# Linear attention beside a gated feed-forward: query features scaled to one normaliser before they are turned, and all sixteen numerators moved among the gate/up chunks

## The chip, the cores and the metric

The kernel runs on one core of one Trainium2 chip. The metric is the device time of one execution in microseconds (us); the median of several runs is what counts. A core has five engines that each work through their own instructions in order and wait for one another by semaphores: TensorE (PE in the profile; its weight loads are PEld), VectorE (DVE), ScalarE (ACT), GpSimd (POOL) and SyncE (SP, which here only issues DMAs). TensorE writes to PSUM, eight banks of 512 f32 columns on 128 rows; all else lives in SBUF, 128 rows as well.

## The reference

Input x is 2048 tokens by 640, bf16. Two branches are computed from it and mixed by a gate per token:

```
g = sigmoid((x * gate_w).sum(-1))
out = g * A(x) + (1 - g) * B(x)

A: q, k, v = x @ wqkv                         32 heads of 20
   pq = q @ w_phi[h],  pk = k @ w_phi[h]      20 x 20 per head
   phi(p) = [softmax(p), softmax(-p)]         40 features
   kv = sum over tokens of phi(pk)^T v        z = sum over tokens of phi(pk)
   o  = (phi(pq) @ kv) / (phi(pq) . z + 1e-6)
   A  = o @ wo                                640 x 640
B: (gelu(x @ w_gate) * (x @ w_up)) @ w_down   640 -> 1728 -> 640
```

The attention is linear: all keys go into one state of 40 x 20 per head, and each query then needs one product with this state (the numerator) and one with z (the normaliser).

## The kernel before, in words

Tokens are handled in 16 tiles of 128 and, for the feed-forward, in 4 blocks of 512. A small recorder (`_Sched.op`, `_Sched.dma`) issues every instruction in program order to its engine, and adds the semaphore waits that the named buffers need. So the order of work on each engine is the order in which the Python code calls the methods. All DMAs of weights and all transposing DMAs are issued by SP, in program order, on one queue.

**Loads and constants** (`loads`). x, the weights of v, and parts of the up weights are issued first. GpSimd fills masks and the constant columns: for each slot of the key features `Ek` (L294, L295) and of the query features `Eqt` (L297, L298) it writes ones at the last of each head's 20 columns and in the padding. The last feature's exponent is subtracted from the others beforehand, so it is always exp(0) = 1 and is never computed.

**Attention state** (`attention_state`). TensorE projects v, then folds `w_phi` into the k weights and the q weights (`fold`). The folded weights are evacuated from PSUM in slices by VectorE; slice 3 of the k weights and of the q weights goes over ScalarE to a staging buffer and from there by one GpSimd subtraction (`fold_stage`, L451) into place. After that come k projections (`k_tile`), k and q together (`kq_tile`), their exponentials on ScalarE (`exps`, L549), the norm of the key features on VectorE (`k_norm`: a reduction L628, a reciprocal L636, a product L637) and the sum over tokens on TensorE (`gram`, L646, eleven groups of three heads). The features lie in eleven groups of 128 columns; each group holds 64 columns of exp(p) and 64 of exp(-p), for three heads of 20 and 4 columns of padding. A tile's query features are written to `Eqt`, and a transposing DMA on SP's queue (L595) turns them at once into `Eq`, so that features lie on the rows. In between, SP issues the gate and up weights piece by piece, then the down weights and `wo`.

**Gate and up** (`ffn`, `gateup`). For each block of 512 tokens there are 14 chunks of hidden columns: ten matmuls of 512 columns (gate, then up), a gelu on ScalarE (L809) and a multiply on VectorE (L813). The narrow chunk 13 has gate and up in five matmuls. For the first block the up half of five chunks (2 to 6) has been computed ahead in the attention stage, so those chunks have only five matmuls. The last grams, the state (`kv_state`) and the gates of all tokens (`gates`) lie among the first four chunks. Two PSUM bank pairs, (0, 1) and (6, 7), take turns. In the last block, six chunks run in this form, in banks 2 to 5, and eight as half-row matmuls (`gateup_halves`, L832: 64 rows of the array for gate and 64 for up side by side, then swapped), with numerators 0, 1 and 2 between them.

**Numerators** (`num`). The state matrix `KV` has, for each group of three heads, 66 columns: 20 of kv, one of z and one of ones for each head. The two softmaxes are not yet normalised when the matmuls run, so the 64 rows of exp(p) and the 64 rows of exp(-p) go to two separate outputs: 22 half-row matmuls per tile (`num_mms`, L875). VectorE then has twelve steps per tile (`num_steps`): the ones columns give the two softmax sums; from these come the ratio, the normaliser, its reciprocal, the gate (L893 to L900), two products of 640 columns (L904) and their sum (L906). A transposing DMA (L909) turns the result into `goT`, eight slots.

**Down** (`down_pair`). For two tiles at a time TensorE multiplies hidden rows with `w_down` and the turned attention rows with `wo` (L935, half-row matmuls in pairs), and ScalarE scales the result by the gate (L948) ahead of the store. Numerators 3 to 15 lie between these matmuls, 13 in all.

## Time and profile before

| what | value |
|---|---|
| median of three runs | 282.25 us (281.9 to 282.58) |
| profiled execution, own time | 281.68 us |
| its span | 280.4 us, 7063 instructions |
| granted TensorE clock | 1.00 in every stretch |
| TensorE busy | 276.6 us (99%) |
| VectorE busy | 177.3 us (63%); 19.6 of 20 us from 40 to 80 us |
| ScalarE busy | 106.4 us (38%) |
| GpSimd busy | 14.4 us (5%), 69 instructions |
| attention stage, gate/up stage, down stage | up to 80, 80 to 193, 193 to 278.5 us |

The page has busy times per engine, the span in 40 slices, the DMA queues, the chain of work that ended last, and the costliest groups of instructions. A group's row reads: line, engine, operation, output <- inputs, shape, count | total busy us, mean ns of one | idle time of the engine before them and what ended it. A row of the chain in order of time reads: start, duration, engine, buffer and line, count. A row of the timeline reads: start, duration, engine, line, operation, and in brackets the idle time before it and its releaser. In the table of DMA issues the last number is the median time from issue to landing. Ends of matmuls are modelled, and the spans of GpSimd instructions are rough.

### The profile page before, as it was taken

What the parts mean: (1) busy time and instruction counts of PE and PEld (TensorE: products, weight loads), DVE (VectorE), ACT (ScalarE), POOL (GpSimd) and SP (SyncE); (2) the same over time, 40 slices, a digit from 0 to 9 for tenths busy, and PEclk for the clock granted to TensorE, in tenths of its full rate; (3) what the DMA queues carried; (4) which work ended last, traced back from release to release, by engine and by line L of the source; (5) the groups of instructions that cost most, each with busy time, mean ns of one, the idle gap of its engine ahead of it and who ended that gap; (6) DMA issues with size and microseconds to landing.
All of it is one profiled execution on the core that took longest, in us unless ns stands there. A gap on an engine that the chain in (4) does not pass through costs nothing.

```text
span 280.4 us, 7063 instructions
## 1 busy us (share of the span) xinstructions
PE 276.6 (99%) x2994; PEld 168.1 (60%) x3006; DVE 177.3 (63%) x342; ACT 106.4 (38%) x205; POOL 14.4 (5%) x69
## 2 busy tenths in 40 slices
PE   8999999999999999999999999999999999999997
PEld 4576766666765444444444444445777777777785
DVE  2666999999998524233242234878884883883801
ACT  3347877878783423222323223122112112112021
POOL 7411001101000000000000000000000000000000
DMA  7999069887899910000000000101133142232221
GB/s 217 224 220 189 6 136 165 171 163 146 162 191 273 347 41 0 2 0 0 1 2 0 0 0 2 23 2 26 26 50 108 35 76 56 62 59 66 71 75 47
DMA packets 59994, 24.11 MB, mean 86 GB/s; under 512 B 50874, under 2 KB 59450, under 8 KB 59962
## 3 DMA queue, kind: packets, MB, share of 16 engines
q1 hardware_dynamic: 59296, 23.63, 37.7%
q8 instruction: 23, 0.38, 0.6%
q10 hardware_dynamic: 666, 0.03, 0.2%
q14 instruction: 9, 0.07, 0.1%
HBM read 9.04 MB, written 2.62 MB: 42 GB/s over the span
## 4 chain that ended last, share of the span: by engine, by line
PE 97%; DMA 1%; issue 0%; SPq 0%; ACT 0%
PE ps L466 52%; PE ps L935 29%; PE ps L832 6%; PE ps L610 4%; PE ps L480 2%; PE ps L875 2%; PE ps L646 2%; DMA xtok<-in_A_x_dram 1%; PE ps L406 1%; PE ps L342 0%; SPq L230 0%; ACT outsb L948 0%; PE ps L371 0%
## 5 line engine op out<-in xcount | busy, mean ns | idle before, releaser
L809 ACT ACTIVATE gl<-ps 128x512 bf16<-128x512 f32 x52 | 31.1, 597 | 71.2 <-PE ps L466 56.3
L466 PE MATMUL ps<-xT,wu_sb 128*128 128x512 bf16 x214 | 52.9, 379 | 0.3
L466 PE MATMUL ps<-xT,wg_sb 128*128 128x512 bf16 x214 | 52.7, 379 | 0.3
L466 PE MATMUL ps<-w,xT 128*128 128x368 bf16 (+6 forms) x340 | 51.6, 303 | 0.0
L813 DVE TENSOR_TENSOR hT<-ps,gl 128x512 bf16<-128x512 f32 x34 | 23.4, 691 | 44.5 <-PE ps L466 44.5
L935 PE MATMUL ps<-wd_sb,hT 64*128 64x320 bf16 x648 | 48.2, 296 | 0.0
L948 ACT ACTIVATE outsb<-ps,Gm 128x320 bf16<-128x320 f32 (+2 forms) x31 | 14.6, 516 | 70.3 <-PE ps L935 70.3
L466 PEld LDWEIGHTS ps<-w,xT 128*128 128x128 bf16 x340 | 32.1, 98 | 14.6
L935 PEld LDWEIGHTS ps<-wd_sb,hT 64*128 64x128 bf16 x648 | 30.9, 94 | 11.8
L466 PEld LDWEIGHTS ps<-xT,wu_sb 128*128 128x128 bf16 x220 | 21.5, 98 | 25.6
L466 PEld LDWEIGHTS ps<-xT,wg_sb 128*128 128x128 bf16 x220 | 21.2, 98 | 25.2 <-issue 0.2
L935 PE MATMUL ps<-wo_sb,goT 64*128 64x320 bf16 (+2 forms) x340 | 26.5, 288 | 0.0
L628 DVE TENSOR_REDUCE Dk<-Ek 128x66 f32<-128x1320 bf16 x16 | 24.3, 1520 | 2.3 <-ACT gcol L539 2.3
L637 DVE TENSOR_TENSOR Ek<-Ek,Dk 128x1320 bf16<-128x1320 bf16 x16 | 24.5, 1533 | 0.5
L904 DVE TENSOR_TENSOR O<-ps,RH 128x640 bf16<-128x640 f32 x32 | 24.8, 815 | 0.0
L549 ACT ACTIVATE Ek<-ps 128x627 bf16<-128x627 f32 x32 | 20.5, 693 | 6.0 <-PE ps L610 4.5
L549 ACT ACTIVATE Eqt<-ps 128x627 bf16<-128x627 f32 x32 | 20.6, 704 | 2.4 <-PE ps L466 2.4
L935 PEld LDWEIGHTS ps<-wo_sb,goT 64*128 64x128 bf16 x340 | 15.8, 94 | 5.5
L832 PE MATMUL ps<-xT,wg_sb 64*128 64x512 bf16 x80 | 17.6, 376 | 0.0
L832 PE MATMUL ps<-xT,wu_sb 64*128 64x512 bf16 x80 | 17.6, 376 | 0.0
L935 PE MATMUL ps<-wd_sb,xT 64*128 64x320 bf16 (+2 forms) x270 | 16.0, 269 | 0.0
L893 DVE RECIPROCAL RH<-ps 128x32 f32<-128x32 f32 x16 | 5.7, 356 | 13.4 <-PE ps L875 13.4
(97 smaller groups left out, 222.3 us busy)
## 6 DMA issues: line engine op xcount, KB each, us to landing
out_dram<-outsb SPq DMA_DIRECT2D x7, 320.0 KB, 2.9
wd_sb<-in_B_w_down_dram SPq DMA_DIRECT2D x1, 2080.0 KB, 12.2
wg_sb<-in_B_w_gate_dram SPq DMA_DIRECT2D x5, 224.0 KB, 3.1
wg_sb<-in_B_w_gate_dram SPq DMA_DIRECT2D x5, 192.0 KB, 3.0
wu_sb<-in_B_w_up_dram SPq DMA_DIRECT2D x5, 192.0 KB, 3.9
wo_sb<-in_A_wo_dram SPq DMA_DIRECT2D x1, 800.0 KB, 10.2
xtok<-in_A_x_dram SPq DMA_DIRECT2D x2, 320.0 KB, 3.2
w<-in_A_wqkv_dram SPq DMA_DIRECT2D x4, 160.0 KB, 3.6
```

Source lines behind the costliest of these rows:

```text
L466: self.sc.op("pe", lambda e: e.matmul(self.ps[:, bank * 512 + c0:bank * 512 + c0 + n], lhs, rhs, start=first, stop=fin), reads=reads, writ ...
L549: self.sc.op("act", lambda e: e.activation(dst, src, AF.Exp, scale=scale), reads=[("ps", b), ("ps", b + 1)], writes=[(name, sl, s)])
L610: self.sc.op("pe", lambda e: e.matmul(out, self.xT[:, kt, t * P:(t + 1) * P], self.w3[:, kt, c:c + 2 * n].rearrange("p (r w) -> p r w", w= ...
L628: self.sc.op("dve", lambda e: e.tensor_reduce(self.Dk[:, se, 0, :].rearrange("p (u h) -> p u h", h=self.HG), self.k_view(se), AX.X, ALU.ad ...
L637: sc.op("dve", lambda e: e.tensor_tensor(v, v, R.rearrange("p (u h) -> p u h", h=self.HG).unsqueeze(3).to_broadcast([P, 2 * self.G, self.H ...
L809: self.sc.op("act", lambda e: e.activation(self.gl[:, slot, :], self.bank(bank), AF.Gelu_apprx_tanh), reads=[("ps", bank)], writes=[("gl", ...
L813: self.sc.op("dve", lambda e: e.tensor_tensor(self.hT(b, c), up, self.gl[:, slot, :], ALU.mult), reads=[upk, ("gl", slot)], writes=[("hT", ...
L832: sc.op("pe", lambda e: e.matmul(self.bank(bk), w[a:a + 64, kt, c * P:(c + 1) * P], self.xT[a:a + 64, kt, b * self.BT:(b + 1) * self.BT], ...
L893: dve(lambda e: e.reciprocal(R(0), Dn[1]), rb, [key(0)], guard=old)
L904: dve(lambda e, o=o, f=f, s=s: e.tensor_tensor(o, V[s][:, :, 0:DH], f, ALU.mult), rb[2 * s:2 * s + 2] + [key(6 + s)], [("O", s, sl)], guar ...
L935: sc.op("pe", lambda e: e.matmul(self.bank(bk, w), lhs, rhs, start=opens and x == 0, stop=end and not opens, skip_group_check=True), reads ...
L948: sc.op("act", lambda e: e.activation(dst, self.bank(bk, w), AF.Copy, scale=g), reads=rd, writes=wr)
```

## The change

The query features are no longer turned as they come, unnormalised. They stay in token rows, in a buffer `Eq` with a slot for each of the 16 tiles, and are scaled first: VectorE sums the two sets of 20 exponentials of each head (`q_sums`, two reductions of 660 elements), forms the ratio of the two sums (`q_ratio`: a reciprocal and a product of 33 columns), and GpSimd multiplies the exp(-p) half by this ratio (`q_scale`, 660 elements). Both halves then share one normaliser, and a group's 128 rows can go through one matmul. Then the transposing DMA turns the tile (`q_turn`): tile 0 into a buffer of its own (`Eq0`), tile t into the slot of tile t-1, which has been turned by then.

A numerator has eleven matmuls of 128 rows and 63 columns (the ones columns are gone from `KV`), in PSUM banks 2 and 3, and three VectorE steps: the normaliser, its reciprocal, and one product of 640 columns with gate and reciprocal, from which `goT` is turned. `goT` has twelve slots; the last four tiles use freed slots of `Eq`.

All 16 tiles are now handled inside the gate/up stage: counting chunks from 0 over all four blocks, sums, ratio and scale of tile t come behind chunk 3 + 3t, numerator t behind chunk 8 + 3t, and the turn of tile t+1 is issued just ahead of numerator t (that of tile 0 right behind its scale). From the seventh chunk on three bank pairs take turns. The half-row chunks and the numerators among the down matmuls are gone. GpSimd's constants for the queries become a fill of all 16 tiles of `Eq` with ones, 1408 columns each, in the order `QT` in which the tiles are projected, at the end of `loads`; the fills come ahead of both `fold_stage` instructions on its queue.

```diff
@@ class _Kernel
-    DB = DH + 2
+    DB = DH + 1
-    NEQ = 4
+    NSQ = 4
+    NGO = 12
+    QT = (0, 4, 1, 2, 3) + tuple(range(5, 16))
@@ alloc
-        self.Eq = T("Eq", [P, self.G, S], BF16)
+        self.Eq = T("Eq", [P, NT, self.G * P], BF16)
...
@@ loads
-        for s in range(self.NEQ):
-            pool(lambda e, s=s: e.memset(self.consts(self.Eqt, s, 0), 1.0), [("Eqtc", s)])
-            pool(lambda e, s=s: e.memset(self.consts(self.Eqt, s, 1), 1.0), [("Eqtp", s)])
+        for t in self.QT:
+            pool(lambda e, t=t: e.memset(self.Eq[:, t, :], 1.0), [("Er", t, 0), ("Er", t, 1)])
@@ q_rest
-        sl = self.nq % self.NEQ
-        self.nq += 1
-        self.exps(self.Eqt, sl, "Eqt", (b + 2) * 512 - (self.H * self.E - n))
-        self.sc.dma("sp", lambda e: e.dma_start_transpose(self.Eq[:, :, t * P:(t + 1) * P], self.Eqt[:, sl, :]),
-                    reads=[("Eqt", sl, 0), ("Eqt", sl, 1), ("Eqtc", sl), ("Eqtp", sl)], writes=[("Eq", t)])
+        self.exps(self.Eq, t, "Er", (b + 2) * 512 - (self.H * self.E - n))
+    def q_sums(self, t):
...
+        for s in (0, 1):
+            sc.op("dve", lambda e: e.tensor_reduce(
+                self.Dq[:, sl, s, :].rearrange("p (g h) -> p g h", h=HG), u[:, s], AX.X, ALU.add),
+                reads=[("Er", t, s)], writes=[("Dq", sl, s)], guard=old)
+    def q_ratio(self, t):
...
+        self.sc.op("dve", lambda e: e.reciprocal(b, b), writes=[("Dq", sl, 1)])
+        self.sc.op("dve", lambda e: e.tensor_tensor(b, a, b, ALU.mult), reads=[("Dq", sl, 0)], writes=[("Dq", sl, 1)])
+    def q_scale(self, t):
...
+        self.sc.op("pool", lambda e: e.tensor_tensor(
+            v, v, ratio.unsqueeze(3).to_broadcast([P, G, HG, self.DH]), ALU.mult),
+            reads=[("Dq", sl, 1)], writes=[("Er", t, 1)])
+    def turned(self, t):
+        return self.Eq[:, t - 1, :] if t else self.Eq0[:, :]
+    def q_turn(self, t):
+        self.sc.dma("sp", lambda e: e.dma_start_transpose(
+            self.turned(t).rearrange("p (g q) -> p g q", q=P), self.Eq[:, t, :]),
+            reads=[("Er", t, 0), ("Er", t, 1)], writes=[("Eq", t)],
+            guard=[("Er", t - 1, s) for s in (0, 1)] if t else ())
@@ kv_state
-        ones = KV[:, :, :, self.DH + 1]
-        sc.op("dve", lambda e: e.tensor_copy(ones, m.unsqueeze(1).to_broadcast([P, self.G, self.HG])),
-              reads=["hm"], writes=["KVd"])
-    def gateup_halves(self, b, cs, pairs, held):
...
@@ num
+        for g in range(self.G):
+            n, o = min(w, H * DB - w * g), base + w * g
+            sc.op("pe", lambda e: e.matmul(
+                self.ps[:, o:o + n], self.turned(t)[:, g * P:(g + 1) * P], self.KV[:, g, 0:n], start=True, stop=True),
+                reads=[("Eq", t)] + [(k, g0) for k in ("KV", "KVz") for g0 in (0, 8, 10)],
+                writes=[("ps", o // 512)], signal=g in (5, self.G - 1))
...
+        sc.op("dve", lambda e: e.scalar_tensor_tensor(
+            R(0), self.Dq[:, t % self.NSQ, 0, 0:H], 1e-6, V[:, :, DH], ALU.mult, ALU.add),
+              reads=rb + [("Dq", t % self.NSQ, 0)], writes=[key(0)], guard=old)
+        sc.op("dve", lambda e: e.reciprocal(R(1), R(0)), reads=[key(0)], writes=[key(1)], guard=old)
+        sc.op("dve", lambda e: e.scalar_tensor_tensor(
+            self.Og[:, sl, :].rearrange("p (h d) -> p h d", d=DH), V[:, :, 0:DH], self.Gr[:, t:t + 1],
+            R(1).unsqueeze(2).to_broadcast([P, H, DH]), ALU.mult, ALU.mult),
+            reads=rb + [key(1), "Gr"], writes=[("Og", sl)], guard=old)
...
@@ ffn
+        two, three = [(0, 1), (6, 7)], [(4, 5), (0, 1), (6, 7)]
         order = [0, 1, 13] + list(range(2, 13))
+        top, step = 8, 3
+        n = 0
+        for b in range(self.NB):
             for idx, c in enumerate(order):
+                self.gateup(b, c, two[n % 2] if n < 6 else three[(n + 1) % 3])
+                if b == 0 and idx < 4:
+                    self.gram(12 + idx)
+                    if idx == 3:
+                        self.kv_state()
+                        self.gates()
+                t, r = divmod(n - 3, step)
+                if 0 <= t < self.NT and r == 0:
+                    self.q_sums(t)
+                    self.q_ratio(t)
+                    self.q_scale(t)
+                    if t == 0:
+                        self.q_turn(0)
+                t, r = divmod(n - top, step)
+                if 0 <= t < self.NT and r == 0:
+                    if t + 1 < self.NT:
+                        self.q_turn(t + 1)
+                    self.num(t, 2)
+                n += 1
...
```

More of the change, by code (lines that the diff above doesn't have):

```diff
@@ L197, in alloc @@
             [("Ek", [P, self.NSE, self.G * P], BF16), ("vaug", [P, self.NSV, self.G, 64], BF16)],
-            [("hT1", [P, NFC, BT], BF16), ("upc", [P, 2, BT], F32), ("RH", [P, 2, 8, self.H], F32)],
+            [("hT1", [P, NFC, BT], BF16), ("RH", [P, 2, 2, self.H], F32), ("Dq", [P, self.NSQ, 2, self.G * self.HG], F32)],
         ])
         place([
-            [("Eqt", [P, self.NEQ, self.G * P], BF16), ("Dk", [P, self.NSE, 2, 2 * self.G * self.HG], F32)],
+            [("Eq0", [P, self.G * P], BF16), ("Dk", [P, self.NSE, 2, 2 * self.G * self.HG], F32)],
             [("hT2", [P, NFC, BT], BF16)],
@@ L209, in alloc @@
             [("under", [P, 4464], F32), ("upf", [P, len(self.UP), BT], F32)],
-            [("goT", [P, 8, KD, P], BF16), ("O1", [P, 2, D], BF16), ("O2", [P, 2, D], BF16),
-             ("Og", [P, 2, D], BF16), ("outsb", [P, 4, D], BF16)],
+            [("goT", [P, self.NGO, KD, P], BF16), ("Og", [P, 2, D], BF16), ("outsb", [P, 4, D], BF16)],
         ])
@@ L591, in q_rest @@
         self.proj(t, c - n, n, b + 2, 0, ["wq2", "wq2t"])
-        sl = self.nq % self.NEQ
-        self.nq += 1
-        self.exps(self.Eqt, sl, "Eqt", (b + 2) * 512 - (self.H * self.E - n))
-        self.sc.dma("sp", lambda e: e.dma_start_transpose(self.Eq[:, :, t * P:(t + 1) * P], self.Eqt[:, sl, :]),
-                    reads=[("Eqt", sl, 0), ("Eqt", sl, 1), ("Eqtc", sl), ("Eqtp", sl)], writes=[("Eq", t)])
+        self.exps(self.Eq, t, "Er", (b + 2) * 512 - (self.H * self.E - n))
+    def q_sums(self, t):
+        sc, HG, sl = self.sc, self.HG, t % self.NSQ
+        u = self.Eq[:, t, :].rearrange("p (g s w) -> p s g w", s=2, w=64)[:, :, :, 0:HG * self.DH].rearrange(
+            "p s g (h f) -> p s g h f", f=self.DH)
+        old = [(w, k) for w in ("vaug", "vmain", "vone") for k in (0, 1, 2)]
+        for s in (0, 1):
+            sc.op("dve", lambda e: e.tensor_reduce(
+                self.Dq[:, sl, s, :].rearrange("p (g h) -> p g h", h=HG), u[:, s], AX.X, ALU.add),
+                reads=[("Er", t, s)], writes=[("Dq", sl, s)], guard=old)
@@ new lines, in q_ratio @@
+    def q_ratio(self, t):
+        sl = t % self.NSQ
+        a, b = [self.Dq[:, sl, s, :] for s in (0, 1)]
+        self.sc.op("dve", lambda e: e.reciprocal(b, b), writes=[("Dq", sl, 1)])
+        self.sc.op("dve", lambda e: e.tensor_tensor(b, a, b, ALU.mult), reads=[("Dq", sl, 0)], writes=[("Dq", sl, 1)])
+    def q_scale(self, t):
+        G, HG, sl = self.G, self.HG, t % self.NSQ
+        v = self.Eq[:, t, :].rearrange("p (g s w) -> p g s w", s=2, w=64)[:, :, 1, 0:HG * self.DH].rearrange(
+            "p g (h f) -> p g h f", f=self.DH)
+        ratio = self.Dq[:, sl, 1, :].rearrange("p (g h) -> p g h", h=HG)
+        self.sc.op("pool", lambda e: e.tensor_tensor(
+            v, v, ratio.unsqueeze(3).to_broadcast([P, G, HG, self.DH]), ALU.mult),
+            reads=[("Dq", sl, 1)], writes=[("Er", t, 1)])
@@ new lines, in turned, with go @@
+    def turned(self, t):
[5 more added lines that the diff above has]
+            guard=[("Er", t - 1, s) for s in (0, 1)] if t else ())
+    def go(self, t):
+        if t < self.NGO:
+            return self.goT[:, t, :, :], ()
+        u = t - self.NGO
+        slot, w = u // 2, self.D * (u % 2)
+        return self.Eq[:, slot, w:w + self.D].rearrange("p (k q) -> p k q", q=P), [("Eq", slot + 1)]
@@ L736, in attention_state @@
             self.k_norm(t)
-        nk, nv, ng, nq = 4, 9, 0, 0
-        self.nq, self.half = 0, 1
+        nk, nv, ng = 4, 9, 0
+        nq, self.half = 0, 1
         pieces = self.gate_pieces()
@@ L818, in gateup_evac @@
         self.gateup_mult(b, c, slot, up, upk, old)
-    def gateup_halves(self, b, cs, pairs, held):
-        sc, KD = self.sc, self.KD
-        old, later = [("xT", t) for t in range(12)], []
-        for close in (0, 1):
-            for c, banks in zip(cs, pairs):
-                i = 0 if c < 7 else 1
-                for kt in range(KD):
-                    for r in (0, 1):
-                        w, wk, bk = ((self.wg_sb, "wg", banks[0]), (self.wu_sb, "wu", banks[1]))[r ^ close]
-                        key = self.upheld(c)[1] if c in self.UP + self.LATE and wk == "wu" else (wk, i, kt)
-                        a, end = 64 * r, kt == KD - 1
-                        sc.op("pe", lambda e: e.matmul(
-                            self.bank(bk), w[a:a + 64, kt, c * P:(c + 1) * P],
-                            self.xT[a:a + 64, kt, b * self.BT:(b + 1) * self.BT], start=close == 0 and kt == 0,
-                            stop=close == 1 and end, skip_group_check=True),
-                            reads=[("xT", t) for t in range(4 * b, 4 * b + 4)] + [key],
-                            writes=[("ps", bk)] + ([("turn", bk)] if end else []), signal=end,
-                            after=[("turn", bk)] if close and kt == 0 else ())
-                if close:
-                    slot = self.gn % 3
-                    self.gn += 1
-                    up, upk = self.bank(banks[1]), ("ps", banks[1])
-                    if c in held:
-                        k = held.index(c)
-                        self.gelu(banks[0], slot)
-                        sc.op("dve", lambda e: e.tensor_copy(self.upc[:, k, :], up), reads=[upk], writes=[("upc", k)],
-                              guard=self.oldk)
-                        later.append(lambda c=c, k=k, slot=slot: self.gateup_mult(
-                            b, c, slot, self.upc[:, k, :], ("upc", k), old))
-                        if len(held) == 1:
-                            later.pop()()
-                    else:
-                        self.gateup_evac(b, c, banks[0], slot, up, upk, old)
-        return later
@@ L856, in before_num, with num @@
     def before_num(self):
         return ([("upf", c) for c in self.UP + self.LATE] + ["kstage", "qstage"] + [("wref", k, h) for k in (0, 3) for h in (0, self.HM)] + [("wref", k, 0) for k in (1, 2, 4)] + [("xtok", k) for k in range(4)] + ["wkT", "wqT"] + self.oldk)
-    def num(self, t, banks=(0, 6)):
+    def num(self, t, b):
+        sc = self.sc
         old = self.before_num()
-        w = self.HG * self.DB
-        base = [b * 512 + 512 - 6 * w for b in banks]
-        self.num_mms(t, base)
-        rb = [("ps", b + k) for b in banks for k in (0, 1)]
-        self.num_steps(t, base, rb, old)
@@ L867, in num_mms @@
-    def num_mms(self, t, base):
-        sc, w = self.sc, self.HG * self.DB
-        for g in range(self.G):
-            n = min(w, self.H * self.DB - w * g)
-            for s in (0, 1):
-                a, o = 64 * s, base[s] + w * g
-                edge = o // 512 != (o + w) // 512
-                first = g == 0 or (o - w) // 512 != o // 512
-                sc.op("pe", lambda e: e.matmul(
-                    self.ps[:, o:o + n], self.Eq[a:a + 64, g, t * P:(t + 1) * P], self.KV[a:a + 64, g, 0:n],
-                    start=first, stop=edge or g == self.G - 1, skip_group_check=True),
-                    reads=[("Eq", t), "KVd"] + [(k, g0) for k in ("KV", "KVz") for g0 in (0, 8, 10)], writes=[("ps", o // 512)],
-                    signal=edge or g == self.G - 1)
@@ L881, in num_steps @@
-    def num_steps(self, t, base, rb, old):
-        sc = self.sc
-        DB, DH, H = self.DB, self.DH, self.H
-        sl = t % 2
-        V = [self.ps[:, base[s]:base[s] + H * DB].rearrange("p (h c) -> p h c", c=DB) for s in (0, 1)]
-        Z = [v[:, :, DH] for v in V]
-        Dn = [v[:, :, DH + 1] for v in V]
+        w, DB, DH, H = self.HG * self.DB, self.DB, self.DH, self.H
+        base, sl = b * 512 + 512 - 6 * w, t % 2
+        for g in range(self.G):
+            n, o = min(w, H * DB - w * g), base + w * g
[3 more added lines that the diff above has]
+                writes=[("ps", o // 512)], signal=g in (5, self.G - 1))
@@ L888, in num_steps @@
+        rb = [("ps", b), ("ps", b + 1)]
+        V = self.ps[:, base:base + H * DB].rearrange("p (h c) -> p h c", c=DB)
         R = lambda k: self.RH[:, sl, k, :]
         key = lambda k: ("RH", sl, k)
-        def dve(fn, reads, writes, guard=()):
-            sc.op("dve", fn, reads=reads, writes=writes, guard=guard)
-        dve(lambda e: e.reciprocal(R(0), Dn[1]), rb, [key(0)], guard=old)
-        dve(lambda e: e.tensor_tensor(R(1), Dn[0], R(0), ALU.mult), rb + [key(0)], [key(1)])
-        dve(lambda e: e.tensor_tensor(R(2), Z[1], R(1), ALU.mult), rb + [key(1)], [key(2)])
@@ L896, in num_steps @@
-        dve(lambda e: e.tensor_tensor(R(3), Z[0], R(2), ALU.add), rb + [key(2)], [key(3)])
-        dve(lambda e: e.scalar_tensor_tensor(R(4), Dn[0], 1e-6, R(3), ALU.mult, ALU.add), rb + [key(3)], [key(4)])
-        dve(lambda e: e.reciprocal(R(5), R(4)), [key(4)], [key(5)])
-        dve(lambda e: e.tensor_scalar(R(6), R(5), self.Gr[:, t:t + 1], None, op0=ALU.mult), [key(5), "Gr"], [key(6)])
-        dve(lambda e: e.tensor_tensor(R(7), R(6), R(1), ALU.mult), [key(6), key(1)], [key(7)])
-        for s, dst in ((0, self.O1), (1, self.O2)):
-            o = dst[:, sl, :].rearrange("p (h d) -> p h d", d=DH)
-            f = R(6 + s).unsqueeze(2).to_broadcast([P, H, DH])
-            dve(lambda e, o=o, f=f, s=s: e.tensor_tensor(o, V[s][:, :, 0:DH], f, ALU.mult),
-                rb[2 * s:2 * s + 2] + [key(6 + s)], [("O", s, sl)], guard=old)
@@ L906, in num_steps @@
-        dve(lambda e: e.tensor_tensor(self.Og[:, sl, :], self.O1[:, sl, :], self.O2[:, sl, :], ALU.add),
-            [("O", 0, sl), ("O", 1, sl)], [("Og", sl)], guard=old)
-        gs = t % 8
-        sc.dma("sp", lambda e: e.dma_start_transpose(self.goT[:, gs, :, :], self.Og[:, sl, :]),
-               reads=[("Og", sl)], writes=[("goT", gs)], guard=old)
+        sc.op("dve", lambda e: e.scalar_tensor_tensor(
+            R(0), self.Dq[:, t % self.NSQ, 0, 0:H], 1e-6, V[:, :, DH], ALU.mult, ALU.add),
+              reads=rb + [("Dq", t % self.NSQ, 0)], writes=[key(0)], guard=old)
@@ new lines, in num @@
+        sc.op("dve", lambda e: e.reciprocal(R(1), R(0)), reads=[key(0)], writes=[key(1)], guard=old)
[3 more added lines that the diff above has]
+            reads=rb + [key(1), "Gr"], writes=[("Og", sl)], guard=old)
+        dst, dead = self.go(t)
+        sc.dma("sp", lambda e: e.dma_start_transpose(dst, self.Og[:, sl, :]), reads=[("Og", sl)],
+               writes=[("goT", t)], guard=old + list(dead))
@@ L925, in mm @@
             t, w0, w = parts[h][j]
-            tt, gs, bk, a = t % 4, t % 8, banks[h][j], 64 * r
+            tt, bk, a = t % 4, banks[h][j], 64 * r
             end = x == n - 1
@@ L932, in mm @@
                 k = c - NFC - 1
-                lhs, rhs = self.goT[a:a + 64, gs, k, :], self.wo_sb[a:a + 64, k, w0:w0 + w]
-                rd = [("goT", gs), "wo"]
+                lhs, rhs = self.go(t)[0][a:a + 64, k, :], self.wo_sb[a:a + 64, k, w0:w0 + w]
+                rd = [("goT", t), "wo"]
             sc.op("pe", lambda e: e.matmul(self.bank(bk, w), lhs, rhs, start=opens and x == 0, stop=end and not opens,
@@ L944, in evac @@
                 rd, wr = [("ps", bk), "Gm"], [("outsb", t % 4, h, j)]
+                was = [("outsb", t % 4, k, (t - t0)) for k in (0, 1)] if last and h < 2 else ()
                 if last and j == 1:
-                    sc.op("dve", lambda e: e.tensor_scalar(dst, self.bank(bk, w), g, None, op0=ALU.mult), reads=rd, writes=wr)
-                else:
-                    sc.op("act", lambda e: e.activation(dst, self.bank(bk, w), AF.Copy, scale=g), reads=rd, writes=wr)
+                    sc.op("dve", lambda e: e.tensor_scalar(dst, self.bank(bk, w), g, None, op0=ALU.mult), reads=rd, writes=wr,
+                          guard=was)
+                else:
+                    sc.op("act", lambda e: e.activation(dst, self.bank(bk, w), AF.Copy, scale=g), reads=rd, writes=wr,
+                          guard=was)
             os_ = t0 % 4
@@ L981 @@
         (w, k) for w in ("vaug", "vmain", "vone") for k in range(9)]
-    oldq = [("Eqt", k, s) for k in range(4) for s in (0, 1)] + [(w, k) for w in ("Eqtc", "Eqtp") for k in range(4)] + [
-        (w, k) for w in ("Dk", "Rk") for k in range(5)]
+    oldq = [("Eq", 0)] + [(w, k) for w in ("Dk", "Rk") for k in range(5)]
     oldw = [(w, k) for w in ("wv", "wk2", "wk2t", "wq2", "wq2t") for k in range(5)] + ["wgate", "wv0"]
@@ L987, in ffn @@
         self.gn = 0
-        self.pn = 0
-        pairs = [(0, 1), (6, 7)]
+        two, three = [(0, 1), (6, 7)], [(4, 5), (0, 1), (6, 7)]
         order = [0, 1, 13] + list(range(2, 13))
-        def gateups(b, after):
+        top, step = 8, 3
+        n = 0
+        for b in range(self.NB):
             for idx, c in enumerate(order):
-                self.gateup(b, c, pairs[self.pn % 2])
-                self.pn += 1
-                after(idx)
-        def downs(b, side):
-            p = [(2, 3), (4, 5)]
-            n = 0
-            for t in (4 * b, 4 * b + 2):
-                final = t + 2 == self.NT
-                for _ in self.down_pair(t, p + [(0, 1)] if final else p, final):
-                    n += 1
-                    if n in side:
-                        self.num(side[n])
@@ L1009, in state @@
-        def state(idx):
-            if idx < 4:
-                self.gram(12 + idx)
-            if idx == 3:
-                self.kv_state()
-                self.gates()
-        def none(idx):
-            pass
-        def last_gateups(b):
-            middle, n = [(2, 3), (4, 5)], 6
-            for idx in range(n):
-                self.gateup(b, order[idx], middle[idx % 2])
-            self.num(0)
-            for g, banks in enumerate((middle, pairs, pairs, middle)):
-                cs = order[n + 2 * g:n + 2 * g + 2]
-                later = self.gateup_halves(b, cs, banks, (cs[:0], cs, cs[:0], cs[:1])[g])
-                if g == 1:
-                    self.num(1, (2, 4))
-                for f in later:
-                    f()
-            self.num(2)
@@ L1032, in ffn @@
-        at = [(None, 36, 66, 96)] + [(1, 31, 61, 91)] * 3
-        gateups(0, state)
-        gateups(1, none)
-        gateups(2, none)
-        last_gateups(3)
-        for b in range(self.NB):
-            downs(b, {at[b][k]: 4 * b + 2 + k for k in range(4 if b < 3 else 2)})
+                self.gateup(b, c, two[n % 2] if n < 6 else three[(n + 1) % 3])
[4 more added lines that the diff above has]
+                        self.gates()
@@ L1041, in bass_gated_mix__linear_kernel_hedgehog__geglu_ffn__prompt_kernel @@
+        p = [(2, 3), (4, 5)]
+        for t in range(0, self.NT, 2):
+            final = t + 2 == self.NT
+            for _ in self.down_pair(t, p + [(0, 1)] if final else p, final):
+                pass
 def bass_gated_mix__linear_kernel_hedgehog__geglu_ffn__prompt_kernel(
```

## The prediction

> **What bounds the kernel now.** I read the busy shares first, then the chain that ended last, then that chain in order of time, and last the queues the change loads: GpSimd (POOL), VectorE (DVE) and the DMA issues.

> ```profile
> PE 276.6 (99%) x2994; PEld 168.1 (60%) x3006; DVE 177.3 (63%) x342; ACT 106.4 (38%) x205; POOL 14.4 (5%) x69
> ...
> PE 97%; DMA 1%; issue 0%; SPq 0%; ACT 0%
> ```

> TensorE is busy from end to end, and the chain is TensorE for 97%. In time order it shows no hole from 5 us on, and what a piece costs:

> ```profile
> 17.98 4.15 PE ps L466 x30
> ...
> 33.34 0.30 PE ps L646 x11
> ...
> 87.83 7.34 PE ps L466 x34
> 95.23 10.74 PE ps L466 x49
> ...
> 175.25 0.43 PE ps L875 x22
> 175.68 8.64 PE ps L832 x80
> 184.32 0.32 PE ps L875 x22
> ...
> 198.50 0.32 PE ps L875 x22
> 198.83 4.08 PE ps L935 x60
> ```

> A numerator (L875) takes 0.32 to 0.33 us, its first 0.43. The gram of one tile (L646), 11 matmuls of 128 rows and 61 columns, takes 0.30: the form the new numerators have. The four half-row chunks (L832, 80 matmuls) take 8.64, 2.16 a chunk; a whole-row chunk takes 10.74 over 49 recorded matmuls of 50, 2.16 too (a record is missing). So the bound is array time, and only two things move the end: array time, or a hole in TensorE's in-order queue. The rest of the reading is on who could make such a hole.

> POOL in order of time:

> ```profile
> 0.80 0.20 POOL L240 MEMSET gz<- 128x128 bf16 x1 [0.29 <-POOLq L1068]
> 0.94 0.20 POOL L243 MEMSET ident<- 128x128 bf16 x1
> ...
> 1.61 0.11 POOL L269 MEMSET mask<- 128x7 bf16 x1
> ...
> 8.21 0.48 POOL L297 MEMSET Eqt<- 128x66 bf16 x1
> ...
> 18.41 0.98 POOL L451 TENSOR_TENSOR w<-kstage 128x475 bf16<-128x475 f32 x1 [8.47 <-ACT wref L435]
> ```

> POOL idles 8.47 us ahead of 18.41, and the subtraction there (part of the folded k weights) feeds TensorE's first k projection. What VectorE and the DMA queue charge for the first numerator's new chain:

> ```profile
> L628 DVE TENSOR_REDUCE Dk<-Ek 128x66 f32<-128x1320 bf16 x16 | 24.3, 1520 | 2.3 <-ACT gcol L539 2.3
> ```

> ```profile
> Eq<-Eqt SPq DMA_TRANSPOSE x16, 3.6
> goT<-Og SPq DMA_TRANSPOSE x16, 2.6
> ```

> **Array time.** Sixteen numerators of 22 half-row matmuls at about 0.325 us (5.2 in all) become sixteen of 11 at the gram's 0.30 to 0.31, with 63 columns in place of 61, say 0.31: 5.0. The half-row chunks become whole-row ones at the same 2.16. The extra 0.1 of the first numerator (0.43) is the first turn to half rows and falls to the first down matmul instead. Net -0.25 us; ends -0.4 and 0.

> **The memsets.** Eight small Eqt memsets go (POOL would be free for the next at 8.21). Sixteen of 128x1408 come, ahead of the L451 subtraction on POOL's queue. No row has this size. Between 7 and 128 elements in a row the duration grows from 0.11 to 0.20 us, 0.8 ns an element; the start spacing of the two 128-element ones is 0.14, leaving about 0.036 an instruction. So 1408 elements take 1.18 us, and 16 end at 8.21 + 18.9 = 27.1. Then L451 (0.98) ends at 28.1. TensorE wants it where k projection 0 reaches weight slice 3: 30 matmuls from 17.98 end at 22.13, that projection has the last ten (3045 columns; at 0.216 us for 512 that is 1.29 us), and its fourth matmul, behind three of 369 columns, starts at 21.3. Behind it in order stand the two up-projections held ahead, the q fold and k tiles 1 to 3, and ScalarE and VectorE wait for those: nobody works ahead. The wait is 28.1 - 21.3 = 6.8 us, all on the path, since nothing behind it has slack to give back. Bounds: nothing, if the 16 end by 20.3 (0.76 us each); above, at the 2.4 ns an element of the short strided memsets (154 elements every 0.375 us), 42 us. I take 6.8: the contiguous 128-element row has the new one's shape. The second L451 (q fold) then finds POOL free and costs nothing; the exponentials that wait for the memsets start at 33.4 before, after their end.

> **The restart.** The only row in which TensorE starts from rest is the beginning:

> ```profile
> L689 PE MATMUL ps<-const-bfloat16-1.0 128*128 128x512 bf16 x6 | 2.7, 626 | 0.8 <-PEq L1068 0.8
> ```

> Six 512-column matmuls last 626 ns each, against 379 later, and start 0.43 apart against 0.216. The slow stretch runs from 0.84 to about 4.0 us (the granted clock in the rows reads 1.00 all the same). No row shows TensorE after a hole inside the kernel, so a restart costs between 0 and half of 3.2 us. For a hole of 6.8 us I take 1.6, from the beginning. For the shorter hole below I take 0, keeping 1.6 as its upper end.
> [...]

> **Numerator 0.** Before, it ran at 175 us with its features long turned. Now it stands behind the ninth chunk, where TensorE arrives at 94.15 (times here are the old ones; the first hole moves all alike). Five of the nine chunks have their up half done, and pass in 1.08 us each. Its features now pass these, from VectorE's end of the gates at 90.9 (0.1 sooner, the ones copy being gone): two reductions of 660 elements at half of L628's stream, 0.83 each, overlapping to 1.6; a reciprocal of 33 columns (0.35 for 32, L898) and a product (0.19), with two gaps of 0.04: done at 93.0. POOL's scaling of 660 elements: L451 takes 0.98 for 475, so 1.33, done at 94.4. The transposing DMA: 3.6 to landing, issue 0.1 later: 98.1. TensorE waits 4.0 us. Bounds: 3.0, if it lands in 2.6 like the smaller goT, and 4.8 at the longest landing of Eq, 4.3. Behind the waiting matmuls stand all later chunks; ScalarE and VectorE run dry after two multiplies. It is on the path.
> [...]

> **The other numerators.** Three chunks and a numerator take 6.8 us. VectorE has in it three multiplies (2.1), sums and ratio (2.2) and the steps on PSUM (0.19, 0.35 and 0.82, some 1.5 with gaps): 5.8. Its multiplies run up to 0.8 late, and a bank pair now comes back only after three chunks, so TensorE does not see it. Turn t+1 is issued with numerator t and lands 3.6 later, against 6.8 to its use. Cost nothing; if VectorE's cover went (7 us where there are 6.8) each would cost the excess, 3 us over sixteen. The round with the narrow chunk is the tightest: 5.7 us for TensorE, about 6.0 to 6.5 for VectorE, made good in the next round.

> **What leaves.** Sixteen Eq transposes leave SP's queue between 35 and 83 us, so weight loads pass earlier; TensorE never waited for them: nothing. VectorE's twelve small steps and two wide products in the down stage were hidden beside TensorE: nothing. The held chunks' copies also: nothing. The output's last steps stay as they are.

> **Sum.** -0.25 + 6.8 + 1.6 + 4.0 = +12.15 us on the profiled execution's 281.68 (span 280.4 and 1.28 around it): 293.8. The median of the runs is 0.57 above that execution, so 294.4 in its terms.

> **Rivals.**
> A, the forecast: both holes, 290.5 to 296.5; 0.70.
> B, the memsets are quick: POOL writes two elements where the 128-element rows show one, 0.6 us each, done by 17.8, ahead of L451's inputs at 18.41. Hole and restart go: 281.7 - 0.25 + 4.0 = 285.4, 286 on the median. For it: spans on POOL are rough. Against it: four rows lie on the 0.8 line. 0.13.
> C, more holes: VectorE, 86% full in the gate/up stage, becomes the bound (3 us), or the shorter hole restarts cold too (1.6) or POOL is shut out (0.7): 296.5 to 299. For it: the round with the narrow chunk. 0.10.
> D, POOL at the strided rate: over 300, to 330. 0.02.
> E, not slower. It needs TensorE to find numerator 0's features turned. Its one mechanism is the length of that chain: 2.1 us of VectorE, POOL's scaling and the landing must fit between 90.9 and 94.15, and with the quick POOL of case B (0.7 for the scaling), which the first hole's absence needs anyway, the landing would have to take under 0.5 us; the smallest landing of a transpose here is 2.6. From there on the time is 281.4 to 282, array time alone. 0.04; the gain in array time is too small to make more than half of this count as faster.
> F, that the change does not do what it says: nothing speaks for it, as the order of the instructions has every memset ahead of L451 and each turn ahead of its numerator. 0.01.

> **Range and chances.** The likeliest is A at 294.4, its own range 290.5 to 296.5. To leave out no more than 2 in 10, and with both ends of the memset price in doubt, I go down to B and up to C: 285.5 to 298.5. What a measurement can tell here is about 0.2% (0.56 us). Faster: half of E, 0.02. Same: the rest of E and F, 0.03. Slower: A to D, 0.95.

> **What would show it.** In the changed profile: sixteen POOL memsets of 128x1408 at about 1.18 us from start to start, ending near 27, and L451 behind them; a hole of TensorE of 6 to 8 us near 21, released by POOL; behind it some 3 us in which 512-column matmuls start 0.43 apart; a hole of about 4 us ahead of the first numerator near 102, released by a transposing DMA; numerators of 0.31; no other hole until the down stage, which is about 4.2 us shorter without its 13 numerators. Memsets at half the time, or TensorE at full rate after the first hole, would make me wrong by 8 and 1.6 us; so would holes that come back at each numerator, as VectorE's row would then be full from 100 to 210 us.

## The result and the profile after

The changed kernel takes 296.72 us in the median (296.61 to 297.17, four runs), the kernel before 282.36 in the same comparison: a ratio of 1.0514, 95% interval 1.0496 to 1.0532. So it is 14.4 us slower, where 12.2 had been forecast. The profiled execution took 297.17 us with a span of 295.9, which is 15.5 over the span before.

From the page of the changed kernel, the busy shares, the granted TensorE clock in 40 slices of 7.4 us, and the chain that ended last:

```profile
PE 280.8 (95%) x2734; PEld 169.3 (57%) x2750; DVE 168.0 (57%) x274; ACT 106.4 (36%) x205; POOL 53.6 (18%) x93
...
PEclk9997799999999989999999999999999999999999
...
PE 82%; POOL 10%; issue 6%; DMA 1%; ACT 0%; POOLq 0%; SPq 0%
```

TensorE no longer fills the span, POOL has come into the chain with 10%, and in two places the clock row shows less than full rate; before, the granted clock was 1.00 throughout. The chain in order of time (start, duration, what) says where:

```profile
8.34 19.40 POOL Eq L298 x16
27.74 0.95 POOL w L451
28.73 1.80 PE ps L466 x7
...
35.09 7.95 PE ps L466 x60
...
102.69 1.69 POOL Eq L616
104.47 3.55 DMA Eq<-Eq
108.07 0.70 PE ps L865 x11
108.77 0.22 issue
108.99 7.70 PE ps L466 x29
116.69 0.31 PE ps L865 x11
...
213.34 80.66 PE ps L908 x1258
```

The sixteen fills run from 8.34 to 27.74, the k fold's subtraction follows, and only then TensorE goes on. At 104.47 the first turn starts, at 108.07 the first numerator. After that the chain is TensorE alone: numerators of 0.31 us, and a down stage of 80.7 (84.9 before, with thirteen numerators in it). The timeline gives the two holes in brackets:

```profile
18.29 3.39 PE L466 MATMUL ps<-w,xT 128*128 128x408 bf16 x23
28.73 1.80 PE L466 MATMUL ps<-w,xT 128*128 128x369 bf16 x7 [7.05 <-POOL w L451]
...
108.07 0.70 PE L865 MATMUL ps<-KV,Eq 128*128 128x63 bf16 x11 [4.05 <-DMA Eq<-Eq]
...
112.21 1.24 PE L466 MATMUL ps<-xT,wg_sb 128*128 128x512 bf16 x5
```

And the stretches of one microsecond around them (stretch, its length, busy time and instructions of each engine, then the granted clock, the DMA share and GB/s):

```profile
25.00:26.00 1.00, 0.00 (x0) 0.00 (x0) 0.00 (x0) 0.00 (x0) 1.00 (x2) 1.00 0.79 113
26.00:27.00 1.00, 0.00 (x0) 0.00 (x0) 0.00 (x0) 0.00 (x0) 1.00 (x2) 0.62 1.26 282
...
32.00:33.00 1.00, 1.00 (x4) 0.42 (x3) 1.00 (x1) 0.30 (x1) 0.00 (x0) 0.50 0.86 277
33.00:34.00 1.00, 1.00 (x9) 0.30 (x9) 0.53 (x1) 0.30 (x1) 0.00 (x0) 0.97 0.37 120
...
107.00:108.00 1.00, 0.00 (x0) 0.00 (x0) 0.93 (x4) 0.00 (x0) 0.28 (x1) 1.00 0.43 81
108.00:109.00 1.00, 0.71 (x12) 0.66 (x14) 0.97 (x3) 0.00 (x0) 1.00 (x1) 0.58 0.00 0
109.00:110.00 1.00, 1.00 (x3) 0.45 (x3) 0.93 (x3) 0.00 (x0) 0.41 (x1) 0.50 0.00 0
...
111.00:112.00 1.00, 1.00 (x5) 0.36 (x4) 0.00 (x0) 0.54 (x1) 0.00 (x0) 0.72 1.14 215
```

The stretch from 26 to 27 reads 0.62, which is 0.76 us of it at half rate, so the clock falls to 0.50 at 26.24, inside the first hole. Reckoned the same way, it comes back at 33.06, falls again at 108.16, when TensorE has just resumed after the second hole, and comes back at 111.56.

For the loss of the profiled execution I take starts of the same work before and after. In the kernel before, these are a row of TensorE's timeline and one of the chain:

```profile
17.91 4.22 PE L466 MATMUL ps<-w,xT 128*128 128x408 bf16 x30
...
25.39 7.95 PE ps L466 x60
```

The opening is 0.38 us later, before anything changed (the first of 30 matmuls starts at 18.29 against 17.91). Then the k projection of tile 1 starts at 35.09 against 25.39, 9.70 late: less 0.38 and the hole of 7.05, the half rate behind the hole cost 2.27. Then the second hole, 4.05, and behind it 4.14 us from numerator 0 to the end of the next chunk (112.21) where 0.31 + 2.16 belong: 1.67. Together 15.4, of the 15.5. A saving of 0.25 in array time would leave 15.2, so some 0.3 us are not placed by this sum.

### The profile page after: what moved, and what is told of

It is laid out like the page before. It is cut to its first block, busy times and chain, and to the rows that moved or that the text cites. A ratio compares the mean times of both kernels' runs of the same rounds, so it can differ in the third digit from the quotient of the medians.

```text
span 295.9 us, 6510 instructions
## 1 busy us (share of the span) xinstructions
PE 280.8 (95%) x2734; PEld 169.3 (57%) x2750; DVE 168.0 (57%) x274; ACT 106.4 (36%) x205; POOL 53.6 (18%) x93
## 4 chain that ended last, share of the span: by engine, by line
PE 82%; POOL 10%; issue 6%; DMA 1%; ACT 0%; POOLq 0%; SPq 0%
PE ps L466 48%; PE ps L908 27%; POOL Eq L298 7%; PE ps L648 3%; PE ps L865 2%; DMA Eq<-Eq 1%; PE ps L684 1%; POOL Eq L616 1%; POOL Ek L295 1%; PE ps L406 0%; POOL mask L271 0%; POOL mask L274 0%; POOL w L451 0%; POOL vaug L293 0%; POOL hmask L284 0%
## 5 line engine op out<-in xcount | busy, mean ns | idle before, releaser
L466 PE MATMUL ps<-xT,wu_sb 128*128 128x512 bf16 x251 | 64.3, 387 | 0.4 <-issue 0.2
L466 PE MATMUL ps<-xT,wg_sb 128*128 128x512 bf16 x253 | 63.5, 383 | 0.8 <-issue 0.2
L466 PE MATMUL ps<-w,xT 128*128 128x368 bf16 (+6 forms) x340 | 52.5, 306 | 7.1 <-POOL w L451 7.1
L466 PEld LDWEIGHTS ps<-w,xT 128*128 128x128 bf16 x340 | 32.3, 98 | 22.2 <-POOL w L451 7.4
L466 PEld LDWEIGHTS ps<-xT,wu_sb 128*128 128x128 bf16 x260 | 26.0, 100 | 32.0 <-issue 2.6
L466 PEld LDWEIGHTS ps<-xT,wg_sb 128*128 128x128 bf16 x260 | 24.2, 98 | 26.9 <-issue 1.0
L616 POOL TENSOR_TENSOR Eq<-Eq,Dq 128x660 bf16<-128x660 bf16 x16 | 21.5, 1345 | 92.9 <-DVE Dq L609 92.9
L666 DVE TENSOR_REDUCE Dk<-Ek 128x66 f32<-128x1320 bf16 x16 | 24.3, 1521 | 10.3 <-ACT gcol L539 10.3
L601 DVE TENSOR_REDUCE Dq<-Eq 128x33 f32<-128x660 bf16 x32 | 25.2, 829 | 0.0
L549 ACT ACTIVATE Eq<-ps 128x627 bf16<-128x627 f32 x32 | 20.6, 705 | 2.4 <-PE ps L466 2.4
L298 POOL MEMSET Eq<- 128x1408 bf16 x16 | 19.6, 1358 | 0.0
L908 PE MATMUL ps<-wo_sb,goT 64*128 64x320 bf16 x240 | 19.3, 296 | 0.0
L877 DVE SCALAR_TENSOR_TENSOR Og<-ps,Gr,RH 128x640 bf16<-128x640 f32 x16 | 14.1, 884 | 0.7
```

The costliest lines, as they stand in the source:

```text
L298: pool(lambda e, t=t: e.memset(self.Eq[:, t, :], 1.0), [("Er", t, 0), ("Er", t, 1)])
L466: self.sc.op("pe", lambda e: e.matmul(self.ps[:, bank * 512 + c0:bank * 512 + c0 + n], lhs, rhs, start=first, stop=fin), reads=reads, writ ...
L549: self.sc.op("act", lambda e: e.activation(dst, src, AF.Exp, scale=scale), reads=[("ps", b), ("ps", b + 1)], writes=[(name, sl, s)])
L601: sc.op("dve", lambda e: e.tensor_reduce(self.Dq[:, sl, s, :].rearrange("p (g h) -> p g h", h=HG), u[:, s], AX.X, ALU.add), reads=[("Er", ...
L616: self.sc.op("pool", lambda e: e.tensor_tensor(v, v, ratio.unsqueeze(3).to_broadcast([P, G, HG, self.DH]), ALU.mult), reads=[("Dq", sl, 1) ...
L666: self.sc.op("dve", lambda e: e.tensor_reduce(self.Dk[:, se, 0, :].rearrange("p (u h) -> p u h", h=self.HG), self.k_view(se), AX.X, ALU.ad ...
```

## The experiments

**The fills shortened to the constant columns.**

```diff
         for t in self.QT:
-            pool(lambda e, t=t: e.memset(self.Eq[:, t, :], 1.0), [("Er", t, 0), ("Er", t, 1)])
+            pool(lambda e, t=t: e.memset(self.consts(self.Eq, t, 0), 1.0), [("Er", t, 0), ("Er", t, 1)])
+            pool(lambda e, t=t: e.memset(self.consts(self.Eq, t, 1), 1.0), [("Er", t, 0), ("Er", t, 1)])
```

> The changed kernel, but GpSimd fills only the constant columns of each query tile (two short memsets of 66 and 88 columns, as the kernel before did for its four slots) in place of the whole 1408. Theory (the fill's length ahead of the k fold makes the first hole): 16 pairs at 0.375 us, as the Ek pairs take, end at 8.2 + 6.0 = 14.2, ahead of the staging at 18.1; the first hole (7.05 us) and its half-rate stretch (2.3) go, the second hole (4.05 to 4.2) with its half-rate stretch (1.7) stays: 296.7 - 9.35 = 287.4 us. Rival (the first hole is only met later: another wait, such as the weights or x tiles that share the DMA engines with the early weight loads, ends last next): the hole shrinks to some 1 to 5 us, 289 to 294. Rival (the fill is not what GpSimd's subtraction waits for): 296.7.

Measured: 287.97 us (287.48 to 288.77; ratio to the kernel before 1.0215, 1.0197 to 1.0233). POOL's timeline, and TensorE's at numerator 0:

```profile
16.77 0.39 POOL L298 MEMSET Eq<- 128x66 bf16 x1
17.22 0.17 POOL L299 MEMSET Eq<- 128x88 bf16 x1
18.58 0.98 POOL L452 TENSOR_TENSOR w<-kstage 128x475 bf16<-128x475 f32 x1 [1.19 <-ACT wref L436]
...
98.52 0.75 PE L866 MATMUL ps<-KV,Eq 128*128 128x63 bf16 x11 [4.03 <-DMA Eq<-Eq]
```

The subtraction now waits for ScalarE, not for the fills, and the first hole is gone with its half rate: 8.75 us of the 9.35 expected. The fills end at 17.4, not at 14.2, only 1.2 us ahead of need: I gave both memsets of a tile the same buffer names, so the second waits for the first, 0.565 us a tile. The second hole stands as it was (4.0, released by the turning DMA), and its half rate varies: the profiled execution, the slowest, has a mean clock of 0.988, the other three 0.994. Neither rival holds: no next wait showed up behind the fills.

**Every numerator one chunk later.**

```diff
-        top, step = 8, 3
+        top, step = 9, 3
```

> The changed kernel, but every numerator and turn one chunk later (numerator t behind chunk 9 + 3t); nothing else. Theory (the second hole is a fixed chain that TensorE reaches too early, and only a hole of some 4 us or more halves the clock): numerator 0 is reached 2.16 us later, the hole is 4.05 - 2.16 = 1.9 us, too short for the half rate, so 2.16 + 1.67 = 3.8 us go: 292.9. Rival (the restart is paid after any hole, in proportion to it or whole): the gain is 2.2 to 3.0, so 293.7 to 294.5. Rival (the last numerator now lies against the down stage and makes a hole there, or numerators at this place wait for their turn): no gain, 296 or more.

Measured: 293.43 us (292.92 to 293.74), 3.3 us less than the changed kernel in the median and 3.7 between the two profiled executions (3.8 expected, 2.2 to 3.0 by the first rival). TensorE's timeline at numerator 0:

```profile
108.36 0.48 PE L865 MATMUL ps<-KV,Eq 128*128 128x63 bf16 x11 [1.87 <-DMA Eq<-Eq]
108.69 1.24 PE L466 MATMUL ps<-xT,wg_sb 128*128 128x512 bf16 x5
109.76 1.24 PE L466 MATMUL ps<-xT,wu_sb 128*128 128x512 bf16 x5
```

The hole is 1.87, near the 4.05 - 2.16 that a fixed chain predicts, and the matmuls behind it start 1.08 us apart by five, at full rate. All four executions have a clock of 0.988, the share of the first hole alone. There is no hole at the down stage, so the second rival is out.

**Four of the sixteen fills behind the q fold.**

```diff
-        for t in self.QT:
+        for t in self.QT[:12]:
             pool(lambda e, t=t: e.memset(self.Eq[:, t, :], 1.0), [("Er", t, 0), ("Er", t, 1)])
...
         self.fold("q", ...)
+        for t in self.QT[12:]:
+            sc.op("pool", lambda e, t=t: e.memset(self.Eq[:, t, :], 1.0), writes=[("Er", t, 0), ("Er", t, 1)])
```

> The changed kernel, but only the first twelve of the sixteen fills stand ahead of the k fold's subtraction on GpSimd's queue; the other four come behind the q fold's. Theory (the hole goes by the fills ahead, 1.21 us each, and a hole well below 4 us leaves the clock at full rate): first hole 7.05 - 4.85 = 2.2 us, no half rate behind it: 296.7 - 4.85 - 2.3 = 289.6. Rival (the slow stretch behind the hole is the cost of any restart): 291.9. Rival (the four late fills hold up something of their own, the q exponentials of the last tiles or the key constants): over 290 in the first case, with a wait of ScalarE or VectorE on GpSimd between 37 and 45 us.

Measured: 292.21, 292.11 and 292.09 us, and one execution of 290.22. The hole is 2.49, where 2.2 had been expected. But the half rate came all the same (TensorE's row behind the hole, then the stretches):

```profile
23.93 1.00 PE L466 MATMUL ps<-w,xT 128*128 128x369 bf16 x7 [2.49 <-POOL w L451]
...
23.00:24.00 1.00, 0.07 (x1) 0.07 (x2) 0.00 (x0) 0.00 (x0) 0.87 (x1) 1.00 0.66 122
24.00:25.00 1.00, 1.00 (x9) 0.74 (x10) 0.00 (x0) 0.00 (x0) 0.00 (x0) 1.00 1.27 290
25.00:26.00 1.00, 1.00 (x4) 0.36 (x3) 0.00 (x0) 0.97 (x2) 0.00 (x0) 0.61 0.80 177
26.00:27.00 1.00, 1.00 (x4) 0.43 (x3) 0.61 (x1) 0.68 (x3) 0.00 (x0) 0.50 1.53 78
...
28.00:29.00 1.00, 1.00 (x19) 0.30 (x19) 0.00 (x0) 0.19 (x1) 0.00 (x0) 0.69 1.27 290
```

TensorE resumes at 23.93 at full rate; at about 25.2, 1.3 us into its work, the clock falls to a half, and returns at about 28.6. So my 'well below 4 us leaves the clock alone' is wrong, and the rival's 291.9 was nearer. The fast execution is no noise: its mean clock is 0.994, the others' 0.988. One stretch of half rate less makes 1.9 us here. Which of the two holes went without it there, this kernel can't say. The four late fills held nothing up.

**Both repairs.** Constant columns alone, and numerators two chunks later:

```diff
-        top, step = 8, 3
+        top, step = 10, 3
...
-        p = [(2, 3), (4, 5)]
+        p = [(4, 5), (2, 3)]
```

> Both repairs: constant columns only, and every numerator two chunks later (behind chunk 10 + 3t), with the down stage's first bank pair changed so that it does not wait for the last numerator's banks. Theory (the two holes are the whole loss, and the array time is 0.25 us less than before): no hole over 0.5 us: 282.4 - 0.25 + 0.2 = 282.3 us, no measurable difference from the kernel before (281.9 to 282.7). Rival (VectorE, 86 per cent full among the chunks, costs something there that the holes have hidden, or the last numerators press on the down stage): 283 to 286. Rival (the array time gains more than its columns, for numerators no longer break the down stage): 280 to 281.5.

Measured: 281.67 us (281.47 to 282.26, eleven runs) against 281.98 of the kernel before (281.67 to 282.42, fifteen runs): a ratio of 0.9993, interval 0.9984 to 1.0002. Its chain is TensorE without a hole:

```profile
88.01 10.80 PE ps L467 x50
98.81 0.31 PE ps L866 x11
99.12 6.48 PE ps L467 x30
...
197.44 0.31 PE ps L866 x11
197.75 80.70 PE ps L909 x1258
```

The two holes and the half rate behind them were the whole loss. VectorE's added work among the chunks costs nothing that shows. What is left of the change itself is -0.3 us with an interval that touches zero, so this version does not measurably beat the kernel before.

**One hole of chosen length.** With both repairs as a base, the first n full fills ahead of the k fold and the others behind the q fold (the same edit as above, with n for 12), and for n = 16 all ahead.

> The kernel with both repairs as a base, so that only the first hole is left, and with a hole of chosen length: 11 full fills ahead of the k fold's subtraction, the other five behind the q fold's. Base 281.7 us. Hole by the fills: 1.21 less than the 2.49 seen with twelve: 1.3 us. Theory (the clock falls by whole windows of 3.4 us, each costing 1.7 us, and only when the hole is long enough for one): no window, 281.7 + 1.3 = 283.0 in every execution. Rival (any hole can drop the clock, by the place at which it falls): some executions at 284.7.

> As the run with eleven, with twelve fills ahead: hole 2.5 us. Theory (one window of 3.4 us at half rate in most executions, none in some, by where the hole falls against the window): 281.7 + 2.5 + 1.7 = 285.9, single executions at 284.2, nothing between, and a granted clock of 0.994 or 1.00 with it. Rival (the spread seen with twelve fills came from the second hole): all executions alike.

> As the run with eleven, with fourteen fills ahead: hole 2.5 + 2.4 = 4.9 us. Theory: always at least one window, 281.7 + 4.9 + 1.7 = 288.3, some executions with two at 290.0 (granted clock 0.994 and 0.988). Rival (the restart grows with the hole, 2.3 for 7.05): 281.7 + 4.9 + 1.6 = 288.2 in all, no second level.

> The changed kernel with the second repair alone: all sixteen fills ahead, numerators behind chunk 10 + 3t. Theory (the holes are independent): 296.7 - 4.2 - 1.7 = 290.8, which is also 281.7 + 7.05 + 2.15. Rival (the two holes share a cost): 289 or 292.

Measured; the hole is that of the one profiled execution of each version, taken over for the others, and the last column is time less 281.7 less the hole:

| fills ahead | hole, us | executions, us (mean granted clock) | left over, us |
|---|---|---|---|
| none (both repairs) | 0 | 281.67 median (1.00) | - |
| 11 | 1.1 | 282.99 to 283.04, five (1.00) | 0.2 |
| 12 | 2.0 | 284.20, 284.24, 284.24 (1.00) | 0.5 |
| 12 | 2.0 | 285.92 (0.994) | 2.2 |
| 14 | 4.8 | 288.36 (0.994) | 1.9 |
| 14 | 4.8 | 289.07, 289.31, 289.44 (0.988) | 2.6 to 2.9 |
| 16 | 7.2 | 290.80, 290.95, 291.52 (0.988) | 1.9 to 2.6 |
| 16 | 7.2 | 291.83 (0.982) | 2.9 |

The mean clock takes steps of 0.006, which is 0.006 x 285 x 2 = 3.4 us at half rate each time, never a part of it. The hole of 1.1 us never brought a step, so the rival for eleven (some executions at 284.7) did not show. With twelve fills one execution in four had a step, with fourteen each had one or two, with sixteen two or three. For twelve the two expected levels came out, 284.2 and 285.9, but the other way round: most executions had been expected at 285.9. The rival for twelve (all executions alike) is out. For fourteen the level of one such 3.4 us came out (288.36 for 288.3), and that of two lay at 289.1 to 289.4, not at 290.0.

The 2.0 of the execution at 285.92 is not its own. In the profiled execution with twelve fills TensorE came to the 30 matmuls ahead of the hole at 18.50, against 18.09 in the version with both repairs. GpSimd sets when TensorE goes on, so a later arrival shortens the hole and leaves the time as it is; this is 0.4 of the 0.5 left over. The execution with the step may so have had a hole of up to about 2.5, as the earlier run with twelve fills had (2.49). TensorE's rows in the profiled execution with twelve, where the clock stayed at 1.00:

```profile
23.88 1.00 PE L466 MATMUL ps<-w,xT 128*128 128x369 bf16 x7 [1.99 <-POOL w L451]
24.94 2.10 PE L466 MATMUL ps<-xT,wu_sb 128*128 128x512 bf16 x9
```

Seven matmuls take 1.00 us there; behind the hole of 7.05 above, the same seven took 1.80. With fourteen fills, where TensorE resumes at 26.36 and the clock has fallen at 25.18 (TensorE's row, then the stretches):

```profile
26.36 1.80 PE L466 MATMUL ps<-w,xT 128*128 128x369 bf16 x7 [4.82 <-POOL w L451]
...
25.00:26.00 1.00, 0.00 (x0) 0.00 (x0) 0.00 (x0) 0.00 (x0) 1.00 (x2) 0.59 0.89 97
26.00:27.00 1.00, 0.65 (x3) 0.33 (x4) 0.00 (x0) 0.00 (x0) 0.30 (x1) 0.50 1.23 254
...
32.00:33.00 1.00, 1.00 (x46) 0.80 (x47) 0.00 (x0) 0.60 (x1) 0.00 (x0) 1.00 0.84 262
```

Here 6.8 us are at half rate, 1.2 of them inside the hole, where they cost nothing: 5.6 / 2 = 2.8, against 2.9 in the table for this execution. The rival for fourteen (a restart that grows with the hole, without levels) is ruled out: the loss behind 7.2 us is no larger than behind 4.8, since more of the half rate falls into the hole (2.5 us of 6.8 in the hole of 7.05 of the changed kernel, from 26.24 to 28.73). With sixteen fills the second repair alone gives 291.23 (290.80 to 291.83), where 290.8 was expected, nearer to that than to the rival's 289 or 292: no cost that the two holes share is seen.

## Why the prediction was right

Its order of steps stands: both holes lay where it put them, with the releasers that it named, and each went in a run that took its cause away. The forecast of 294.4 was 2.3 below the median; two sizes made nearly all of that, both of the restart. So the measured 296.7 lies just above the 290.5 to 296.5 of case A, the likeliest, and inside case C, which had been given 0.10: of C it was the clause that the shorter hole restarts cold too that came true.

- **Array time.** Forecast -0.25 us. A numerator takes 0.31, as the gram row said; the version without holes measures -0.3 (interval from -0.5 to +0.1). Right, as far as it can be told.
- **The fills.** Forecast 1.18 us each, end at 27.1; measured 19.40 / 16 = 1.21, end at 27.74. The slope from the rows of 7 and 128 elements carried to 1408 (the forecast's own figures, 0.8 ns an element and 0.036 us, make 1.16). The hole was 7.05 for 6.8: GpSimd's subtraction ended 0.6 later than forecast and TensorE stopped 0.4 later, so the two errors partly cancel. It went when the fills were shortened.
- **The restart behind it.** Forecast 1.6 from the opening rows, measured 2.3. This is the first term that was mis-sized. The half rate lasted 6.8 us (26.24 to 33.06), of which 4.3 fell on work; I had taken one stretch of 3.2. And the clause that the granted clock does not show it holds for the opening only: inside the kernel the rows read 0.50.
- **Numerator 0.** Forecast 4.0, measured 4.05. Sums and ratio took 2.15 (forecast 2.1), the landing 3.55 (3.6). The scaling took 1.68 for 1.33. In the forecast's times, which are 9.70 us earlier here, the turn landed at 98.3 for 98.1 and TensorE arrived at 94.3 for 94.15: two small errors cancel, so the closeness of the sum is partly luck. The hole shrank to 1.87 when the numerator came one chunk later, and was gone with two.
- **The restart behind that.** I took 0 and kept 1.6 as the upper end; measured 1.67. This is the second term. The step that failed is the sentence that took nothing for the shorter hole: rows of the opening say how deep and how long the half rate is, but not behind how long a hole it comes, and I had chosen the length of the hole as the reason without a row. The two restarts together had 1.6 in the forecast and cost 3.9. A hole of 2.49 us (four fills behind the q fold) dropped the clock too.
- **The other numerators, and what leaves.** Forecast nothing, and nothing it is: no hole over 0.22 us after numerator 0 in any of the traces. VectorE at 86% of a round did not bind (that part of rival C is out).
- **Rival B** (quick fills) and **D** are out by 1.21 us a fill. **E** (not slower) failed where it was placed: the landing alone took 3.55.

GpSimd's scaling took two lengths. Timeline of the changed kernel around the first and the third:

```profile
102.53 0.69 DVE L848 TENSOR_TENSOR hT<-upl,gl 128x512 bf16<-128x512 f32 x1
102.69 1.68 POOL L616 TENSOR_TENSOR Eq<-Eq,Dq 128x660 bf16<-128x660 bf16 x1 [15.31 <-DVE Dq L609]
...
103.13 2.39 DVE L848 TENSOR_TENSOR hT<-upf,gl 128x512 bf16<-128x512 f32 x2
...
115.14 0.69 DVE L848 TENSOR_TENSOR hT<-ps,gl 128x512 bf16<-128x512 f32 x1
115.30 1.30 POOL L616 TENSOR_TENSOR Eq<-Eq,Dq 128x660 bf16<-128x660 bf16 x1 [5.90 <-DVE Dq L609]
```

Beside the multiplies of held-up chunks (both inputs in SBUF) the scaling takes 1.68 us, and two such multiplies 2.39 (1.28 in the kernel before, at 91.39); beside multiplies that read PSUM it takes 1.30. The first two scalings are 1.68 and the other fourteen 1.30. Beside the second, at 107.72, the multiply of the held-up chunk takes 0.68, no longer than the 0.69 of such a multiply in the kernel before, at 92.82. The price on the path was some 0.4 us (1.68 - 1.30). The 0.7 that case C has for a POOL that is shut out is shown by no run; these 0.4 are what the rows show in its place. No run took the scaling and the multiplies apart, so what made the difference is not shown by experiment.

## What to carry to other kernels

Where one engine fills the span, a change that moves little of its work is judged by the queues: for each added instruction ask what stands behind it on its own queue, and for each new chain whether its length fits between its inputs and the moment at which the full engine arrives. A constant fill belongs behind the work that something waits for, and the first of a row of software-pipelined steps needs more lead than the later ones, since nothing precedes it. In these runs a hole in TensorE's queue of 2 to 2.5 us or more could cost more than its length, by up to 2.9 us.
